# Keys in 8 MB loads: grouped query attention of one decoded token over a 32,768-row cache

## The chip, the cores and the metric

The kernel runs on one core of a Trainium2 chip. The metric is the device time of one execution in microseconds. A program takes it from three runs (median, lowest, highest); one more execution was recorded by the hardware profiler, and all rows of the profile are from that one.

## The reference

Two batch rows, one new token each. A layer norm of `x` feeds an attention block over a long key and value cache and a small dense block whose output gates it:

```python
xn = layernorm(x)                                  # (2, 1, 512)
q = (xn @ wq).reshape(2, 1, 32, 128)               # 32 query heads
# 8 key heads, each shared by 4 query heads; 32,768 cached rows of 128
scores = q . k_cache * 128 ** -0.5                 # k_cache (2, 8, 32768, 128) float32
o = softmax(scores) . v_cache                      # v_cache (2, 8, 32768, 128) float32
s = o.reshape(2, 1, 4096) @ wo                     # wo (4096, 512)
h = relu(xn @ w1 + b1) ** 2                        # w1 (512, 1792)
g = silu(h @ w2 + b2)                              # w2 (1792, 512)
out = x + s * g
```

All data are float32. The two caches are 268 MB each and make up nearly all of the 561 MB that are read.

## The kernel before

The work is cut into 16 *streams* `s`, one for each pair of key head and batch row, and each stream into 4 *chunks* of 8192 cache rows (4 MB). Chunk `n` is chunk `n % 4` of stream `n // 4`, for n from 0 to 63.

**Loads.** All bulk loads are issued by SP in one fixed order, the list `loads`, from a ring of four buffers of 32 KB for each of the 128 partitions (L56, tag "r"). A load goes out as soon as a buffer is free: `give()` frees one and calls `issue()`, which emits as many loads of the list as there is room for. The order is wq in two halves, then k0, k1, w1, k2, w2, k3, then keys and values in turn (k4, v0, k5, v1, ...), the last four value chunks, and wo in four parts, the last of which goes in four pieces (PIECES). A key load (`load_k`, L91) gives partition p 64 cache rows of 128 floats, one run of 32 KB in the cache; the partitions' runs start 128 KB apart, since all four chunks of a stream interleave by partition. A value load (`load_v`, L98) takes 4 MB in one piece, again with 32 KB for each partition.

**Scores** (`scores(n)`): DVE transposes the key chunk in 32x32 blocks into eight tiles `kt` (L246, eight instructions), PE multiplies them with the stream's queries `qz` (L251) into the PSUM tile `sc[t]`, and DVE takes the maximum (L255). The ring buffer of the keys is free after the eighth transpose. `set_q` (L232, POOL) lays out the queries of a stream.

**Softmax and probabilities.** `softmax(s)` runs after the stream's fourth chunk: the maximum over all (DVE, PE, DVE), then four exponentials on ACT (L272) into the tile `p`. `probs(s)` transposes `p` on PE (L286), copies it to `pT` (L287, ACT) and computes the reciprocals of the sums (L292 to L296). 

**Values** (`values(n)`): PE multiplies `pT` with a value chunk (L309) into `o_ps`. The value buffer is free after these matmuls. After the fourth chunk the stream's output is scaled and laid out (L316 to L329).

The main loop runs `n` from 0 to 67. In step n it emits `scores(n)`; the dense block's first layer in step 1 (`mlp_up`) and its second in step 2 (`mlp_down`); `probs` of the stream before in the first step of a stream; `softmax` of the stream in its fourth; and `values(n - 4)`. So values run four chunks behind scores. At the end PE multiplies with wo (L390), DVE applies the gate and adds x (L399, L400), and two small stores write the result. Each engine executes its instructions in the order in which they were emitted.

Of the kernel before, what the change touches and what calls it, by code (L numbers as in the profile page):

```python
# [9 lines left out]
F32 = mybir.dt.float32  # L10
# [4 lines left out]
P = 128  # L15
# [4 lines left out]

NG = 4
RUN = 64
CHUNK = P * RUN
NO = 16
BUFS = 4
NEG = -3.0e38
PIECES = ((0, 4), (4, 6), (6, 7), (7, 8))

# [2 lines left out]
def gqa_decode_kernel(ctx: ExitStack, tc: tile.TileContext, x, kc, vc, wq, wo, w1, b1, w2, b2, out):  # L33
    nc = tc.nc
    B, _, D = x.shape
# [4 lines left out]
    ND = D // P  # L40
# [11 lines left out]
    out2 = out.rearrange("b s d -> (b s) d")  # L52

    const = ctx.enter_context(tc.tile_pool(name="const", bufs=1))
    ring = ctx.enter_context(tc.tile_pool(name="ring", bufs=BUFS))
    ktpool = ctx.enter_context(tc.tile_pool(name="ktpool", bufs=8))  # L56
    work = ctx.enter_context(tc.tile_pool(name="work", bufs=2))
    pms = ctx.enter_context(tc.tile_pool(name="pms", bufs=2, space=bass.MemoryType.PSUM))
# [3 lines left out]
        return pms.tile([P, 512], F32, tag="ms", name=name)  # L62


    xt = const.tile([P, D], F32, name="xt")
    b1t = const.tile([NG, FG], F32, name="b1t")
    b2t = const.tile([1, D], F32, name="b2t")
    nc.vector.memset(xt, 0.0)
    nc.scalar.dma_start(xt[:B, :], x2)
    nc.scalar.dma_start(b1t, b1.rearrange("(g f) -> g f", g=NG))  # L70
# [8 lines left out]
    def rows(cache, s):  # L79
        hkv, b = divmod(s, B)  # L80
        return cache[b, hkv]

    def load_wq(i):
        t = ring.tile([P, 2, wq.shape[1]], F32, tag="r", name=f"wq{i}")
        nc.sync.dma_start(t, wq.rearrange("(p d) f -> p d f", p=P)[:, 2 * i:2 * i + 2, :])
        return t

    def load_k(m):
        s, u = divmod(m, NCH)
        t = ring.tile([P, RUN, DH], F32, tag="r", name=f"k{m}")  # L90
        nc.sync.dma_start(t, rows(kc, s).rearrange("(p t r) d -> p t r d", p=P, t=NCH)[:, u])  # L91
        return t

    def load_v(m):
        s, u = divmod(m, NCH)
        t = ring.tile([P, RUN, DH], F32, tag="r", name=f"v{m}")
        src = rows(vc, s)[u * CHUNK:(u + 1) * CHUNK].rearrange("(p r) d -> p r d", p=P)
        nc.sync.dma_start(t, src)  # L98
        return t

    def load_w1(_):
        t = ring.tile([P, ND, F], F32, tag="r", name="w1")
        nc.sync.dma_start(t, w1.rearrange("(p d) f -> p d f", p=P))
        return t

    def load_w2(_):
        t = ring.tile([P, FJ, D], F32, tag="r", name="w2")
        nc.sync.dma_start(t, w2.rearrange("(p j) e -> p j e", p=P))
        return t


    def load_wo(i):
        if i % 2 == 0:
            wide[i // 2] = ring.tile([P, 2, WG, D], F32, tag="r", name=f"wo{i // 2}")
        t = wide[i // 2][:, i % 2]
        src = wo[i * WG * P:(i + 1) * WG * P, :].rearrange("(p j) e -> p j e", p=P)
        if i < NWG - 1:
            nc.sync.dma_start(t, src)
        else:
            for j0, j1 in PIECES:  # L120
                nc.sync.dma_start(t[:, j0:j1, :], src[:, j0:j1, :])
        return t

    wide = {}
    NK = NS * NCH
    loads = [(1, load_wq, 0), (1, load_wq, 1)]
    for m in range(NK + NCH):
        if m < NK:
            loads.append((1, load_k, m))
        if m == 1:  # L130
            loads.append((1, load_w1, 0))
        if m == 2:
            loads.append((1, load_w2, 0))
        if m >= NCH:
            loads.append((1, load_v, m - NCH))
    loads += [(1 - i % 2, load_wo, i) for i in range(NWG)]
    free = [BUFS]
    done = [0]

    def issue():  # L140
        while done[0] < len(loads) and free[0] >= loads[done[0]][0]:
            bufs, f, a = loads[done[0]]
            free[0] -= bufs
            tiles[f, a] = f(a)
            done[0] += 1

    def take(f, a):
        return tiles.pop((f, a))

    def give():  # L150
        free[0] += 1
        issue()

    issue()
# [37 lines left out]
    nc.scalar.activation(st[:, 2:3], st[:, 1:2], AF.Sqrt)  # L192
    nc.vector.reciprocal(st[:, 3:4], st[:, 2:3])
    nc.vector.tensor_scalar(xn, xn, st[:, 3:4], None, op0=ALU.mult)  # L194
    xnT = const.tile([P, ND, P], F32, name="xnT")
    t_ps = misc("xnT_ps")
    for d in range(ND):
        nc.tensor.transpose(t_ps[:, d * P:(d + 1) * P], xn.rearrange("p (k d) -> p d k", d=ND)[:, d], ident)  # L198
    nc.vector.tensor_copy(xnT.rearrange("p a b -> p (a b)"), t_ps)  # L199


    for i in range(2):
        wqt = take(load_wq, i)
        for d2 in range(2):
            d = 2 * i + d2
            for f in range(2):
                for g in range(NG):
                    cc = f * NG + g
                    nc.tensor.matmul(sc[f][32 * g:32 * g + 32, :], xnT[:, d, 0:32],  # L209
                                     wqt[:, d2, cc * 512:(cc + 1) * 512], start=(d == 0), stop=(d == ND - 1))  # L210
        give()
    qT = const.tile([P, B, HKV, REP, 4], F32, name="qT")
    for f in range(2):
        for h in range(REP):
# [20 lines left out]
    rm, pr, pT, rs = {}, {}, {}, {}  # L235

    def scores(n):
        s, t = divmod(n, NCH)
        if t == 0:
            rm[s] = work.tile([P, NCH], F32, tag="rm4", name=f"rm4_{s}")  # L240
        kt = take(load_k, n)
        for e0 in range(0, 4, 2):
            kts = []
            for g in range(NG):
                r = ktpool.tile([P, 2, NO, 32], F32, tag="kt", name=f"kt{n}_{e0}_{g}")
                nc.vector.transpose(r.rearrange("p e o w -> p o e w"),  # L246
                                    kt[:, g * NO:(g + 1) * NO, e0 * 32:(e0 + 2) * 32].rearrange("p o (e w) -> p o e w", e=2))
                kts.append(r)
            for e in range(2):
                for g in range(NG):  # L250
                    nc.tensor.matmul(sc[t][32 * g:32 * g + 4 * REP, :], qz[s % 2][:, e0 + e, :],  # L251
                                     kts[g][:, e].rearrange("p o w -> p (o w)"),
                                     start=(e0 + e == 0), stop=(e0 + e == 3))
        give()
        nc.vector.tensor_reduce(rm[s][:, t:t + 1], sc[t], axis=AX.X, op=ALU.max)  # L255

    def softmax(s):
# [21 lines left out]

    def probs(s):  # L280
        p, lh = pr.pop(s)
        sb = work.tile([P, NG, 4, NO, REP], F32, tag="pT", name=f"pT{s}")
# [12 lines left out]
        r4 = work.tile([P, 4, REP], F32, tag="rs", name=f"rs{s}")  # L295
        nc.vector.tensor_mul(r4, selg[:, :4 * REP].rearrange("p (o h) -> p o h", h=REP),  # L296
                             r[:, None, :].to_broadcast([P, 4, REP]))
        rs[s] = r4
# [3 lines left out]
    def values(n):  # L302
# [3 lines left out]
        for i in range(NO // 4):  # L306
            for g in range(NG):
# [1 line left out]
                nc.tensor.matmul(o[32 * g:32 * g + 16, :], pT[s][:, g, a, 4 * i:4 * i + 4, :].rearrange("p o h -> p (o h)"),  # L309
                                 vt[:, lo:lo + 4, :].rearrange("p o d -> p (o d)"),  # L310
                                 start=(a == 0 and i == 0), stop=(a == NCH - 1 and i == NO // 4 - 1))
        give()
        if a == NCH - 1:
            hkv, b = divmod(s, B)
            o_sb = work.tile([P, 512], F32, tag="o_sb", bufs=1, name=f"o_sb{s}")
# [5 lines left out]
            nc.vector.tensor_copy(oT[:, hkv * REP:(hkv + 1) * REP, b], t_ps[:, :REP])  # L321
            if hkv % 2 == 1:
                i = hkv // 2
                m = work.tile([P, WG, P // WG], F32, tag="om", name=f"om{s}")
# [4 lines left out]
                nc.scalar.copy(oW[:, i, :, b], t_ps[:, :WG])  # L329


    hT, gate = const.tile([P, FJ, 32], F32, name="hT"), const.tile([P, DE], F32, name="gate")

    def mlp_up():
        wt = take(load_w1, 0)
# [6 lines left out]
        give()  # L342
# [7 lines left out]
    def mlp_down():  # L350
# [5 lines left out]
        for j in range(FJ):  # L356
            for g in range(NG):
                nc.tensor.matmul(y_ps[32 * g:32 * g + 32, :DE], hT[:, j, :], wt[:, j, g * DE:(g + 1) * DE],  # L358
                                 start=False, stop=(j == FJ - 1))
        give()  # L360
        e = work.tile([P, DE], F32, tag="e", name="e")
        nc.scalar.activation(e, y_ps[:, :DE], AF.Sigmoid)
        nc.vector.tensor_mul(gate, e, y_ps[:, :DE])


    for n in range(NK + NCH):
        s, t = divmod(n, NCH)
        if n < NK:
            if t == 0:
                set_q(s)  # L370
            scores(n)
        if n == 1:
            mlp_up()
        if n == 2:
            mlp_down()
        if s >= 1 and t == 0:
            probs(s - 1)
        if n < NK and t == NCH - 1:
            softmax(s)
        if n >= NCH:  # L380
            values(n - NCH)


    a_ps = sc[0]
# [9 lines left out]
        project(i, 0, WG)  # L394
    for j0, j1 in PIECES:
        project(NWG - 1, j0, j1)
    asb = work.tile([P, DE], F32, tag="e", name="a_sb")
    fin = const.tile([P, DE], F32, name="fin")
    nc.vector.tensor_mul(asb, gate, a_ps[:, :DE])  # L399
    nc.vector.tensor_add(fin, asb, xe)  # L400
# [25 lines left out]
```

## Time and profile before

| | |
|---|---|
| median of 3 runs | 1316.25 us (1316.2 to 1316.35) |
| the profiled execution | 1315.98 us |
| its span, first to last instruction | 1314.2 us |
| granted TensorE clock, mean | 0.861 of full |
| busy: PE, DVE, ACT | 946.4, 675.2, 107.5 us |
| read from HBM | 561.01 MB |

The page gives the span in 40 equal slices, a digit for each engine: its busy share in tenths. A row of instructions reads: line, engine, operation, tiles out<-in, sizes, count; in the timeline it is preceded by its start and its duration in us, and followed in brackets by the idle time ahead of it and what ended that. A name with q (SPq) is the engine's sequencer issuing a DMA. A DMA queue's row gives packets, MB, and the time of its packets as a share of 16 DMA engines. A row "DMA packets" counts all queues and says how many packets were small. The chain of waits goes back from the last instruction, at each step to what released it: its rows give start, duration and what.

### The profile page before, as it was taken

How to read it: one execution, taken by the hardware profiler on the slowest of the kernel's cores; microseconds unless marked ns; L12 is line 12 of the kernel's file. 1: busy time of each engine (PE TensorE's matmuls, PEld its weight loads, DVE VectorE, ACT ScalarE, POOL GpSimd, SP SyncE). 2: the span in 40 equal slices, each digit the busy share in tenths (PEclk: the TensorE clock that was granted, in tenths of full speed). 3: DMA queues.
4: the chain of work that ended last, by engine and by line, in shares of the span. 5: the costliest groups of instructions: out<-in, count | busy, mean ns of one | idle time of the engine just before them, and what ended most of it. 6: DMA issues, size and time to landing. Idle time of an engine off the chain costs nothing.

```text
span 1314.2 us, 11662 instructions
## 1 busy us (share of the span) xinstructions
PE 946.4 (72%) x5054; PEld 245.7 (19%) x5054; DVE 675.2 (51%) x778; ACT 107.5 (8%) x237; POOL 15.1 (1%) x76
## 2 busy tenths in 40 slices
PE   4777786876868677776776778586686767668666
PEld 1121121212112121111212112121211212112123
DVE  4765564553655465465454556355365546446510
ACT  0010000101001010100101001010100101010010
POOL 1000000000000000000000000000000000000000
PEclk9989888988888878887887988898887887888798
DMA  9999999999999999999999999999999999999997
GB/s 412 425 436 430 431 430 430 429 431 431 431 432 431 430 430 430 431 431 430 431 431 430 430 431 430 431 434 430 432 431 432 429 433 432 430 430 432 430 431 310
DMA packets 20113, 561.76 MB, mean 427 GB/s; under 512 B 2247, under 2 KB 2267, under 8 KB 2654
## 3 DMA queue, kind: packets, MB, share of 16 engines
q1 hardware_dynamic: 20024, 561.00, 99.3%
q8 instruction: 39, 0.64, 0.2%
q14 instruction: 12, 0.10, 0.0%
q10 hardware_dynamic: 38, 0.02, 0.0%
HBM read 561.01 MB, written 0.00 MB: 427 GB/s over the span
## 4 chain that ended last, share of the span: by engine, by line
DMA 76%; DVE 22%; PE 1%; issue 0%; ACTq 0%; DVEq 0%
DMA k<-in_A_k_cache 71%; DVE kt L246 22%; DMA v<-in_A_v_cache 2%; DMA wo<-in_A_wo 2%; PE sc L209 1%; DMA xt<-in_A_x 1%; PE y_ps L358 0%; PE sc L251 0%; PE xnT_ps L198 0%; DVE sq L189 0%; DVE xnT L199 0%; DVE st L190 0%; DVE st L186 0%; DVEq L246 0%; ACTq L70 0%
## 5 line engine op out<-in xcount | busy, mean ns | idle before, releaser
L251 PE MATMUL sc<-kt,qz 128*16 128x512 f32 x2048 | 605.6, 695 | 276.9 <-DVE kt L246 256.2
L246 DVE STREAM_TRANSPOSE kt<-k 128x1024 f32<-128x1024 f32 x512 | 584.3, 1207 | 288.3 <-DMA k<-in_A_k_cache 288.3
L309 PE MATMUL o_ps<-v,pT 128*16 128x512 f32 x2048 | 272.9, 604 | 11.5 <-DMA v<-in_A_v_cache 11.5
L251 PEld LDWEIGHTS sc<-kt,qz 128*16 128x16 f32 x2048 | 94.1, 100 | 768.9 <-DVE kt L246 652.0
L272 ACT ACTIVATE p<-sc,nm 128x512 f32<-128x512 f32 x64 | 68.8, 1198 | 1025.4 <-DVE nm L268 1025.4
L255 DVE TENSOR_REDUCE rm<-sc 128x1 f32<-128x512 f32 x64 | 44.3, 692 | 126.3 <-PE sc L251 126.3
L309 PEld LDWEIGHTS o_ps<-v,pT 128*16 128x16 f32 x2048 | 66.1, 98 | 169.9 <-issue 152.0
L286 PE MATMUL pT_ps<-ident,p 128*128 128x128 f32 x256 | 52.1, 381 | 0.1
L286 PEld LDWEIGHTS pT_ps<-ident,p 128*128 128x128 f32 x256 | 46.3, 205 | 5.6 <-issue 2.6
L320 PE MATMUL oT_ps<-rs,o_sb 128*128 128x4 f32 x128 | 19.2, 273 | 34.3 <-ACT o_sb L316 34.3
L275 DVE TENSOR_REDUCE l<-l 128x1 f32<-128x4 f32 x16 | 2.5, 154 | 66.9 <-ACT p L272 66.9
L294 DVE RECIPROCAL r<-l_ps 128x4 f32<-128x4 f32 x16 | 2.9, 183 | 56.5 <-PE l_ps L292 56.5
L321 DVE COPY oT<-oT_ps 128x4 f32<-128x4 f32 x16 | 2.6, 163 | 51.7 <-PE oT_ps L320 51.7
L287 ACT COPY pT<-pT_ps 128x256 f32<-128x256 f32 x64 | 23.9, 373 | 45.7 <-PE pT_ps L286 45.1
L320 PEld LDWEIGHTS oT_ps<-rs,o_sb 128*128 128x128 f32 x128 | 17.8, 215 | 48.3 <-ACT o_sb L316 48.3
L232 POOL COPY qz<-qT 32x16 f32<-32x16 f32 x64 | 12.8, 200 | 1081.4 <-PE sc L251 1051.2
L261 PE MATMUL mx_ps<-ident,rm 128*128 128x128 f32 x16 | 5.1, 319 | 15.8 <-DVE rm L259 15.8
L272 ACT ACTIVATION_READ_ACCUMULATOR p<-sc,nm 128x1 f32 x64 | 14.6, 228 | 0.0
L316 ACT COPY o_sb<-o_ps 128x512 f32<-128x512 f32 x16 | 9.7, 604 | 31.0 <-PE o_ps L309 31.0
L198 PE MATMUL xnT_ps<-ident,xn 128*128 128x128 f32 x4 | 1.1, 428 | 15.2 <-DVE xn L194 15.2
L390 PE MATMUL sc<-wo,oW 128*32 128x128 f32 x256 | 8.8, 275 | 3.4 <-DMA wo<-in_A_wo 3.3
L209 PE MATMUL sc<-wq,xnT 128*32 128x512 f32 x64 | 10.0, 792 | 0.8 <-DVE xnT L199 0.8
(67 smaller groups left out, 107.5 us busy)
## 6 DMA issues: line engine op xcount, KB each, us to landing
k<-in_A_k_cache SPq DMA_DIRECT2D x64, 4096.0 KB, 29.6
v<-in_A_v_cache SPq DMA_DIRECT2D x64, 4096.0 KB, 29.6
wq<-in_A_wq SPq DMA_DIRECT2D x2, 4096.0 KB, 12.2
w<-in_B_w SPq DMA_DIRECT2D x2, 3584.0 KB
wo<-in_A_wo SPq DMA_DIRECT2D x3, 2048.0 KB
wo<-in_A_wo SPq DMA_DIRECT2D x1, 1024.0 KB
wo<-in_A_wo SPq DMA_DIRECT2D x1, 512.0 KB
wo<-in_A_wo SPq DMA_DIRECT2D x2, 256.0 KB, 29.4
```

The costliest lines, as they stand in the source:

```text
L209: nc.tensor.matmul(sc[f][32 * g:32 * g + 32, :], xnT[:, d, 0:32], wqt[:, d2, cc * 512:(cc + 1) * 512], start=(d == 0), stop=(d == ND - 1))
L232: nc.gpsimd.tensor_copy(qz[s % 2][32 * a:32 * a + 32, :, a * REP:(a + 1) * REP], qT[32 * a:32 * a + 32, b, hkv].rearrange("p h e -> p e h"))
L246: nc.vector.transpose(r.rearrange("p e o w -> p o e w"), kt[:, g * NO:(g + 1) * NO, e0 * 32:(e0 + 2) * 32].rearrange("p o (e w) -> p o e w ...
L251: nc.tensor.matmul(sc[t][32 * g:32 * g + 4 * REP, :], qz[s % 2][:, e0 + e, :], kts[g][:, e].rearrange("p o w -> p (o w)"), start=(e0 + e = ...
L255: nc.vector.tensor_reduce(rm[s][:, t:t + 1], sc[t], axis=AX.X, op=ALU.max)
L272: nc.scalar.activation(p[:, :, :, t], sc[t].rearrange("p (o w) -> p o w", w=32), AF.Exp, bias=nm, scale=SCALE, accum_out=l4[:, t:t + 1])
L286: nc.tensor.transpose(t_ps[:, j * P:(j + 1) * P], p[:, 4 * i + j].rearrange("p w t -> p (w t)"), ident)
L287: nc.scalar.copy(sb[:, :, :, 4 * i:4 * i + 4, :].rearrange("p g a o h -> p o g a h"), t_ps.rearrange("p (o g y) -> p o g y", o=4, g=NG)[:, ...
L309: nc.tensor.matmul(o[32 * g:32 * g + 16, :], pT[s][:, g, a, 4 * i:4 * i + 4, :].rearrange("p o h -> p (o h)"), vt[:, lo:lo + 4, :].rearran ...
L316: nc.scalar.copy(o_sb, o)
L320: nc.tensor.matmul(t_ps[:, :REP], o_sb[:, i * DH:(i + 1) * DH], r4[:, i, :], start=(i == 0), stop=(i == 3))
L390: nc.tensor.matmul(a_ps[32 * g:32 * g + 32, :DE], oW[:, i, j, :], wot[i][:, j, g * DE:(g + 1) * DE], start=(i == 0 and j == 0), stop=(i == ...
```

## The change

- The ring goes. Keys get one tile of three slots of 32 KB (`kslots`), values, wq, w1 and w2 a pool of two buffers of 32 KB (`vpool`).
- From the second stream on, keys are loaded two chunks at a time: 8 MB, with one run of 64 KB for each partition. Load m (chunks 2m and 2m + 1) fills slots 0 and 1 when m is even, 1 and 2 when it is odd. The chunk in slot 1, which the next load needs first, is processed first; `TS` says which quarter of a stream's rows a chunk is.
- The first stream's keys are loaded in four halves of such a load (`load_half`, 4 MB, 32 KB runs), with w1 after the second and w2 after the fourth.
- After each 8 MB key load from the third on come two value loads. At the end v60 and v61 go into key slots 0 and 1, and wo into slots 2 and 0.
- A load waits for a named event instead of a count of free buffers: key load m for `("s", 2m - 2)`, the transposes of the first chunk of the load before; value load j for `("v", j - 2)`; the list is still in one order on SP.
- `mlp_down` moves from step 2 to step 3, `probs(s)` from the first step of the next stream to the end of the stream's own fourth step, behind `softmax(s)` and `values(n - 4)`.
- To make room, x, b2, xnT and hT share the memory of the tile `p`, and `pT`, `om` and `e` have one buffer instead of two.

```diff
+TS = (1, 0, 2, 3)
...
-    ring = ctx.enter_context(tc.tile_pool(name="ring", bufs=BUFS))
+    vpool = ctx.enter_context(tc.tile_pool(name="vpool", bufs=2))
...
+    first = work.tile([P, 4, D], F32, tag="p", bufs=1, name="first")
+    xt, b2t = first[:, 0], first[0:1, 1]
...
+    def key_slot(n):
+        return n // 2 % 2 + TS[n % NCH] % 2
+
+    def load_half(n):
+        t = TS[n]
+        nc.sync.dma_start(kslots[:, key_slot(n)], rows(kc, 0).rearrange("(p t r) d -> p t (r d)", p=P, t=NCH)[:, t])
+
     def load_k(m):
-        s, u = divmod(m, NCH)
-        t = ring.tile([P, RUN, DH], F32, tag="r", name=f"k{m}")
-        nc.sync.dma_start(t, rows(kc, s).rearrange("(p t r) d -> p t r d", p=P, t=NCH)[:, u])
-        return t
+        s, u = divmod(m, 2)
+        nc.sync.dma_start(kslots[:, u:u + 2, :].rearrange("p i f -> p (i f)"),
+                          rows(kc, s).rearrange("(p u r) d -> p u (r d)", p=P, u=2)[:, u])
 
     def load_v(m):
         s, u = divmod(m, NCH)
-        t = ring.tile([P, RUN, DH], F32, tag="r", name=f"v{m}")
-        src = rows(vc, s)[u * CHUNK:(u + 1) * CHUNK].rearrange("(p r) d -> p r d", p=P)
-        nc.sync.dma_start(t, src)
+        if m - NK + NCH in (0, 1):
+            t = kslots[:, m - NK + NCH].rearrange("p (r d) -> p r d", d=DH)
+        else:
+            t = vpool.tile([P, RUN, DH], F32, tag="v", name=f"v{m}")
+        nc.sync.dma_start(t, rows(vc, s)[u * CHUNK:(u + 1) * CHUNK].rearrange("(p r) d -> p r d", p=P))
         return t
...
-    loads = [(1, load_wq, 0), (1, load_wq, 1)]
-    for m in range(NK + NCH):
-        if m < NK:
-            loads.append((1, load_k, m))
-        if m == 1:
-            loads.append((1, load_w1, 0))
-        if m == 2:
-            loads.append((1, load_w2, 0))
-        if m >= NCH:
-            loads.append((1, load_v, m - NCH))
-    loads += [(1 - i % 2, load_wo, i) for i in range(NWG)]
+    kslots = const.tile([P, 3, RUN * DH], F32, name="kslots")
+    loads = [(None, load_wq, 0), (None, load_wq, 1), (None, load_half, 0), (None, load_half, 1), (("q", 0), load_w1, 0),
+             (("s", 0), load_half, 2), (None, load_half, 3), (("q", 1), load_w2, 0)]
+    for m in range(2, NK // 2):
+        loads.append((("s", 2 * m - 2), load_k, m))
+        for j in (2 * m - 4, 2 * m - 3):
+            loads.append((("w", j) if j < 2 else ("v", j - 2), load_v, j))
+    loads += [(("s", NK - 3), load_v, NK - 4), (("s", NK - 2), load_v, NK - 3),
+              (("v", NK - 6), load_v, NK - 2), (("v", NK - 5), load_v, NK - 1)]
+    loads += [(("s", NK - 1), load_wo, 0), (("s", NK - 1), load_wo, 1), (("v", NK - 4), load_wo, 2), (("v", NK - 4), load_wo, 3)]
...
-        s, t = divmod(n, NCH)
-        if t == 0:
+        s, t = n // NCH, TS[n % NCH]
+        if n % NCH == 0:
...
-        kt = take(load_k, n)
+        kt = kslots[:, key_slot(n)].rearrange("p (r d) -> p r d", d=DH)
...
-        give()
+        give("s", n)
...
-        if n == 2:
+        if n == NCH - 1:
             mlp_down()
-        if s >= 1 and t == 0:
-            probs(s - 1)
-        if n < NK and t == NCH - 1:
+        if n < NK and i == NCH - 1:
             softmax(s)
         if n >= NCH:
             values(n - NCH)
+        if n < NK and i == NCH - 1:
+            probs(s)
```

More of the change, by code (lines that the diff above doesn't have):

```diff
@@ L26 @@
 NO = 16
-BUFS = 4
+TS = (1, 0, 2, 3)
 NEG = -3.0e38
@@ L62, in misc @@
         return pms.tile([P, 512], F32, tag="ms", name=name)
-    xt = const.tile([P, D], F32, name="xt")
+    first = work.tile([P, 4, D], F32, tag="p", bufs=1, name="first")
+    xt, b2t = first[:, 0], first[0:1, 1]
     b1t = const.tile([NG, FG], F32, name="b1t")
-    b2t = const.tile([1, D], F32, name="b2t")
     nc.vector.memset(xt, 0.0)
@@ L83, in load_wq @@
     def load_wq(i):
-        t = ring.tile([P, 2, wq.shape[1]], F32, tag="r", name=f"wq{i}")
+        t = vpool.tile([P, 2, wq.shape[1]], F32, tag="v", name=f"wq{i}")
         nc.sync.dma_start(t, wq.rearrange("(p d) f -> p d f", p=P)[:, 2 * i:2 * i + 2, :])
         return t
+    def key_slot(n):
[3 more added lines that the diff above has]
+        nc.sync.dma_start(kslots[:, key_slot(n)], rows(kc, 0).rearrange("(p t r) d -> p t (r d)", p=P, t=NCH)[:, t])
     def load_k(m):
-        s, u = divmod(m, NCH)
-        t = ring.tile([P, RUN, DH], F32, tag="r", name=f"k{m}")
-        nc.sync.dma_start(t, rows(kc, s).rearrange("(p t r) d -> p t r d", p=P, t=NCH)[:, u])
-        return t
+        s, u = divmod(m, 2)
+        nc.sync.dma_start(kslots[:, u:u + 2, :].rearrange("p i f -> p (i f)"),
+                          rows(kc, s).rearrange("(p u r) d -> p u (r d)", p=P, u=2)[:, u])
     def load_v(m):
         s, u = divmod(m, NCH)
-        t = ring.tile([P, RUN, DH], F32, tag="r", name=f"v{m}")
-        src = rows(vc, s)[u * CHUNK:(u + 1) * CHUNK].rearrange("(p r) d -> p r d", p=P)
-        nc.sync.dma_start(t, src)
+        if m - NK + NCH in (0, 1):
[3 more added lines that the diff above has]
+        nc.sync.dma_start(t, rows(vc, s)[u * CHUNK:(u + 1) * CHUNK].rearrange("(p r) d -> p r d", p=P))
         return t
     def load_w1(_):
-        t = ring.tile([P, ND, F], F32, tag="r", name="w1")
+        t = vpool.tile([P, ND, F], F32, tag="v", name="w1")
         nc.sync.dma_start(t, w1.rearrange("(p d) f -> p d f", p=P))
@@ L106, in load_w2 @@
     def load_w2(_):
-        t = ring.tile([P, FJ, D], F32, tag="r", name="w2")
+        t = vpool.tile([P, FJ, D], F32, tag="v", name="w2")
         nc.sync.dma_start(t, w2.rearrange("(p j) e -> p j e", p=P))
@@ L113, in load_wo @@
         if i % 2 == 0:
-            wide[i // 2] = ring.tile([P, 2, WG, D], F32, tag="r", name=f"wo{i // 2}")
+            wide[i // 2] = kslots[:, 2 - i].rearrange("p (i j e) -> p i j e", i=2, j=WG)
         t = wide[i // 2][:, i % 2]
@@ L125, in gqa_decode_kernel @@
     NK = NS * NCH
-    loads = [(1, load_wq, 0), (1, load_wq, 1)]
-    for m in range(NK + NCH):
-        if m < NK:
-            loads.append((1, load_k, m))
-        if m == 1:
-            loads.append((1, load_w1, 0))
-        if m == 2:
-            loads.append((1, load_w2, 0))
-        if m >= NCH:
-            loads.append((1, load_v, m - NCH))
-    loads += [(1 - i % 2, load_wo, i) for i in range(NWG)]
-    free = [BUFS]
+    kslots = const.tile([P, 3, RUN * DH], F32, name="kslots")
[8 more added lines that the diff above has]
+    loads += [(("s", NK - 1), load_wo, 0), (("s", NK - 1), load_wo, 1), (("v", NK - 4), load_wo, 2), (("v", NK - 4), load_wo, 3)]
+    past = {None}
     done = [0]
     def issue():
-        while done[0] < len(loads) and free[0] >= loads[done[0]][0]:
-            bufs, f, a = loads[done[0]]
-            free[0] -= bufs
+        while done[0] < len(loads) and loads[done[0]][0] in past:
+            _, f, a = loads[done[0]]
             tiles[f, a] = f(a)
@@ L148, in take, with give @@
         return tiles.pop((f, a))
-    def give():
-        free[0] += 1
+    def give(*event):
+        past.add(event)
         issue()
@@ L194, in gqa_decode_kernel @@
     nc.vector.tensor_scalar(xn, xn, st[:, 3:4], None, op0=ALU.mult)
-    xnT = const.tile([P, ND, P], F32, name="xnT")
+    xnT = first[:, 2].rearrange("p (d b) -> p d b", d=ND)
     t_ps = misc("xnT_ps")
@@ L198, in gqa_decode_kernel @@
         nc.tensor.transpose(t_ps[:, d * P:(d + 1) * P], xn.rearrange("p (k d) -> p d k", d=ND)[:, d], ident)
-    nc.vector.tensor_copy(xnT.rearrange("p a b -> p (a b)"), t_ps)
+    nc.vector.tensor_copy(first[:, 2], t_ps)
     for i in range(2):
@@ L210, in gqa_decode_kernel @@
                                      wqt[:, d2, cc * 512:(cc + 1) * 512], start=(d == 0), stop=(d == ND - 1))
-        give()
+        give("q", i)
     qT = const.tile([P, B, HKV, REP, 4], F32, name="qT")
@@ L253, in scores @@
                                      start=(e0 + e == 0), stop=(e0 + e == 3))
-        give()
+        give("s", n)
         nc.vector.tensor_reduce(rm[s][:, t:t + 1], sc[t], axis=AX.X, op=ALU.max)
@@ L281, in probs @@
         p, lh = pr.pop(s)
-        sb = work.tile([P, NG, 4, NO, REP], F32, tag="pT", name=f"pT{s}")
+        sb = work.tile([P, NG, 4, NO, REP], F32, tag="pT", bufs=1, name=f"pT{s}")
         for i in range(NO // 4):
@@ L311, in values @@
                                  start=(a == 0 and i == 0), stop=(a == NCH - 1 and i == NO // 4 - 1))
-        give()
+        give("v", n)
         if a == NCH - 1:
@@ L323, in values @@
                 i = hkv // 2
-                m = work.tile([P, WG, P // WG], F32, tag="om", name=f"om{s}")
+                m = work.tile([P, WG, P // WG], F32, tag="om", bufs=1, name=f"om{s}")
                 nc.vector.tensor_mul(m, oT[:, i * WG:(i + 1) * WG, b:b + 1].to_broadcast([P, WG, P // WG]),
@@ L329, in values @@
                 nc.scalar.copy(oW[:, i, :, b], t_ps[:, :WG])
-    hT, gate = const.tile([P, FJ, 32], F32, name="hT"), const.tile([P, DE], F32, name="gate")
+    hT, gate = first[:, 3, :FJ * 32].rearrange("p (j b) -> p j b", j=FJ), const.tile([P, DE], F32, name="gate")
     def mlp_up():
@@ L341, in mlp_up @@
                                  start=False, stop=(d == ND - 1))
-        give()
+        give("w", 0)
         hr = work.tile([P, FG], F32, tag="tmp", name="hr")
@@ L359, in mlp_down @@
                                  start=False, stop=(j == FJ - 1))
-        give()
-        e = work.tile([P, DE], F32, tag="e", name="e")
+        give("w", 1)
+        e = work.tile([P, DE], F32, tag="e", bufs=1, name="e")
         nc.scalar.activation(e, y_ps[:, :DE], AF.Sigmoid)
@@ L366, in gqa_decode_kernel @@
     for n in range(NK + NCH):
-        s, t = divmod(n, NCH)
+        s, i = divmod(n, NCH)
         if n < NK:
-            if t == 0:
+            if i == 0:
                 set_q(s)
@@ L396, in gqa_decode_kernel @@
         project(NWG - 1, j0, j1)
-    asb = work.tile([P, DE], F32, tag="e", name="a_sb")
+    asb = work.tile([P, DE], F32, tag="e", bufs=1, name="a_sb")
     fin = const.tile([P, DE], F32, name="fin")
@@ L412 @@
     from concourse.bass_utils import run_bass_kernel_spmd
-    nc = bacc.Bacc("TRN2", target_bir_lowering=False, num_devices=1)
+    nc = bacc.Bacc("TRN2", target_bir_lowering=False, num_devices=1, dynamic_dma_scratch_size=1024)
     arrays, args = {}, {}
```

## The prediction

> **What bounds the kernel now.** I read the page first: the slices, the queues and the chain of waits.
>
> ```profile
> span 1314.2 us, 11662 instructions
> PE   4777786876868677776776778586686767668666
> DVE  4765564553655465465454556355365546446510
> DMA  9999999999999999999999999999999999999997
> q1 hardware_dynamic: 20024, 561.00, 99.3%
> HBM read 561.01 MB, written 0.00 MB: 427 GB/s over the span
> DMA 76%; DVE 22%; PE 1%; issue 0%; ACTq 0%; DVEq 0%
> k<-in_A_k_cache SPq DMA_DIRECT2D x64, 4096.0 KB, 29.6
> ```
>
> No engine fills its row, while the DMA row is full in every slice but the last: q1, the queue of SP's loads, takes 99.3% of the 16 DMA engines' span. The chain's 22% for DVE is misleading. It follows the release of one buffer to the load that refills it, and that load then stands 29.6 us between issue and landing although it moves only 4 MB. The chain in order of time and the transfers of the steady part show why:
>
> ```profile
> 382.42 9.14 DVE kt L246 x8
> 391.57 29.60 DMA k<-in_A_k_cache
> ...
> 1055.15 29.61 DMA k<-in_A_k_cache
> DMA packets 17328, 504.20 MB, mean 431 GB/s; under 512 B 1916, under 2 KB 1916, under 8 KB 1916
> q1 hardware_dynamic: 17283, 503.55, 100.1%
> q8 instruction: 34, 0.56, 0.2%
> ```
>
> The chain steps from one key load to the next but one. Between the two rows shown are 17 such steps, (1055.15 - 391.57)/17 = 39.03 us each; four loads (two of keys, two of values) go in that time, so a load takes 9.76 us. Of the 29.6 us from issue to landing, some 20 are thus spent behind two other loads. The last three rows are the window from 100 to 1270 us: the engines are 100% busy there, and 1916 tiny packets (some 16 for each load) are the only ones under 8 KB. The time is therefore bytes plus whatever each packet costs beside its bytes. The bytes do not change. I need the cost of a packet.
>
> **Price of a packet.** Two windows at the end hold smaller packets (wo in 16, 8, 4 and 2 KB runs):
>
> ```profile
> DMA packets 460, 6.29 MB, mean 419 GB/s; under 512 B 54, under 2 KB 54, under 8 KB 80
> q1 hardware_dynamic: 460, 6.29, 98.6%
> DMA packets 551, 2.39 MB, mean 239 GB/s; under 512 B 67, under 2 KB 67, under 8 KB 425
> q1 hardware_dynamic: 549, 2.36, 58.0%
> q1 hardware_dynamic: 291, 1.05, 51.8%
> DMA  7997967879278165444656536645565744343100
> ```
>
> The first pair is 1285 to 1300 us, the second 1300 to 1310, the single row 1304 to 1309; the last row shows 1300 to 1310 in 40 slices of 0.25 us. Let each data packet cost a, its share of the tiny packets included, and each MB b. Steady window: 100.1% of 16 x 1170 us is 18,739 us for 17283 - 1916 = 15,367 data packets and 503.55 MB. Window 1300 to 1310: 58.0% of 160 us is 92.8 us for 549 - 67 = 482 packets and 2.36 MB. Taken together, b = 37.21 - 30.52a (us per MB), and 482a + 2.36b = 92.8 gives a = 0.0121 us. The window 1285 to 1300 (98.6% of 240 us, 406 packets, 6.29 MB) gives 0.0120. So a data packet costs 12 ns beyond its bytes on the mean engine, within about 1 ns for the rounding of the rows.
>
> The end is not set by the mean engine. From 1304 to 1309 us only 51.8% of the engines' time is used: about half of them have finished the last load and the others have not. The share missing is 1.4% of 15 us in the first window, 0.2 us, and 42% less 1.4 points for an instruction fetch over 10 us, 4.1 us, of which 0.5 lies after the last packet (two empty slices). The last engines end about 3.8 us after the mean. Each engine moves the same bytes in (20024 - 2247)/16 = 1111 data packets (the page has 2247 under 512 B), so if the lag is a packet's cost, it is 3.4 ns each, and the last engines pay 15.4 ns. Against that, records that overlap (100.1% and 0.2%) could make 12 ns too much by 0.3% of the 1219 ns of one packet, 3.7 ns. I take 13.5 ns, between the mean and the last engines, since the last set the end; the bounds are 8.4 and 15.4.
>
> **What the change takes away.** The first stream's four key chunks keep 32 KB runs; the other 60 chunks go in 30 loads of 128 packets of 64 KB instead of 60 loads of 128 packets of 32 KB. That is 30 x 128 = 3840 packets fewer, 240 for each engine: 240 x 13.5 ns = 3.24 us (2.0 to 3.7). There are 30 x 16 tiny packets fewer, 30 for each engine. No view prices them alone; they lie between 0 and a data packet's 12 ns, so 0 to 0.36 us, and I take 0.2. A steady window has no packet over 32 KB. One of 64 KB could cost what two do (gain 0 beside the tiny ones) or one; the three sizes above lie on one line, so I take one. Sum: 3.4 us.
>
> The Trainium skill, "DMA: Bandwidth & Descriptors", section "Why small descriptors are slow (HBM only)", names a fixed overhead of about 3 cycles per packet; at the 850 MHz of its section "Where 436 GB/s comes from" that is an estimate of 3.5 ns, and the sum would be 0.8 us, lost in the noise. The 12 ns of the windows speak against it.
>
> **What it moves: the refill of the keys.** Today any buffer released lets the next 4 MB go. Afterwards an 8 MB key load waits for one thing: the DVE transposes of the first half of the key load before it, which free the middle slot. SP is in order, so both value loads behind it wait as well. Cover is what is queued at that time: the pair of values.
>
> ```profile
> 617.10 9.13 DVE L246 STREAM_TRANSPOSE kt<-k 128x1024 f32<-128x1024 f32 x8 [7.62 <-DMA k<-in_A_k_cache]
> 618.40 9.78 PE L251 MATMUL sc<-kt,qz 128*16 128x512 f32 x32 [6.22 <-DVE kt L246]
> 626.25 0.33 SPq L91 DMA_DIRECT2D k<-in_A_k_cache  x1
> 629.40 3.63 PE L309 MATMUL o_ps<-v,pT 128*16 128x512 f32 x32
> 641.21 0.17 DVE L296 TENSOR_TENSOR rs<-selg,r 128x16 f32<-128x16 f32 x1
> 641.30 9.12 DVE L246 STREAM_TRANSPOSE kt<-k 128x1024 f32<-128x1024 f32 x8
> ```
>
> DVE starts on keys as they land, takes 9.13 us, and SP issues at 626.25, 0.02 us after it. The values cover 2 x 9.76 = 19.5 us, so the new load is in the queue 10.4 us before the DMA engines would run dry. The worst place is the stream's last step, where softmax and now probs stand on DVE ahead of the next transposes. Counted from the landing of that stream's last 8 MB: PE does scores, values and scores, about 1.3 + 9.8 + 3.6 + 9.8 = 24.5 us. From the end of scores (628.18) to the next stream's transposes (641.30) is 13.1 us in the trace, with softmax, values and probs in it as after the change. Sum 37.6 us; the next keys land 39.0 us after the last. DVE is ready just in time, and the 10.4 us are still behind that. The value loads wait for values two loads back, done a whole pair earlier. I cost the refill at nothing; without the cover each us would be paid at up to 15 stream heads.
>
> **Start and end.** The first five loads keep their order, so the third key chunk lands as before:
>
> ```profile
> 0.74 1.98 SPq L85 DMA_DIRECT2D wq<-in_A_wq  x2
> 33.13 9.09 DVE L246 STREAM_TRANSPOSE kt<-k 128x1024 f32<-128x1024 f32 x8
> 42.25 0.33 SPq L108 DMA_DIRECT2D w<-in_B_w  x1
> 61.49 9.13 DVE L246 STREAM_TRANSPOSE kt<-k 128x1024 f32<-128x1024 f32 x8 [0.32 <-DMA k<-in_A_k_cache]
> 72.40 3.22 PE L358 MATMUL y_ps<-w,hT 128*32 128x128 f32 x100
> ```
>
> That chunk waits for the first chunk's transposes (42.2 us) and is wanted at about 61.5 - 9.8 = 51.7: margin 9.5 us. The first 8 MB load waits for the third chunk's transposes, 70.6 us, with the fourth chunk and w2 still to run until 61.5 + 9.8 + 8.5 = 79.8: margin 9.2 us. mlp_down one chunk later frees a value slot needed at 79.8 + 19.5 + 9.8 = 109 us, and ends at about 61.5 + 9.8 + 9.1 + 2 + 4 = 86; the first softmax, whose probabilities now lie where mlp_down reads, is put off by those 4 us, under the 10.4 of cover. At the end the order v, v, v, v, wo stays; v60 and v61 take key slots long free, and the last steps are the same:
>
> ```profile
> 1309.99 0.43 PE L390 MATMUL sc<-wo,oW 128*32 128x128 f32 x8 [0.21 <-DMA wo<-in_A_wo]
> 1310.80 0.29 DVE L400 TENSOR_TENSOR fin<-a_sb,xe 128x128 f32<-128x128 f32 x1
> ```
>
> Both cost nothing. The other edits (the tiles that share space, fewer spare buffers) touch nothing that waits: pT with one buffer is written by probs only after the values that read it, which stand before it in every step; om and e are written 8 and 2 times in all.
>
> The profiled execution took 1315.98 us (span 1314.2 and 1.8 around it), the median is 1316.25. 1315.98 - 3.4 = 1312.6 profiled, and with the 0.27 us between them 1312.8 as the time.
>
> **Rivals.**
> 1. *No packet is saved, or it costs next to nothing.* A 64 KB run goes as two packets, or costs as two. For it: nothing over 32 KB is in the trace. Against it: a packet's cost comes out the same from windows of 16 KB and of mostly 2 to 4 KB. Only the tiny packets go: 1316.25 - 0.2 = 1316.0. By the three cycles of the Trainium skill quoted above the time would be 1315.3; a fifth of this rival's chance is for that.
> 2. *The refill runs dry (slower).* Its place is SP's wait for the middle slot, and it decides when the transposes end over 19.5 us after the landing, 9.1 in the trace: a delay of 10.4 us. Were DVE held for 12 us at each of 15 stream heads, the DMA engines would stand for 15 x 1.6 = 24 us: 1312.8 + 24 = 1337. For it: softmax, values and probs now stand in one piece before a stream's first transposes. Against it: the sum of 37.6 us, and the 7.62 us of idle DVE ahead of its set today.
> 3. *Long runs move slower.* At 1% more for each byte of the 60 chunks, 60 x 9.76 x 1% = 5.9 us are lost and 3.4 won: 1318.7. It decides at 0.6%. For it: each engine then stays in one place of the cache twice as long, which no row here prices. Against it: b is the same in windows of short and of long runs.
> 4. *A load has a cost of its own.* 4.19 MB at b/16 = 2.30 us per MB are 9.66 us, which leaves 0.10 of the 9.76; 8 packets of 12 ns make the same 0.10. What the rounding and the late engines leave is 8 x 4.4 ns = 0.035 us; 30 loads fewer would bring 1.1 us more: 1311.7, and 1311.1 with the upper prices of the packets (3.7 + 0.36 + 1.1 = 5.2). The Trainium skill, same page, section "Anatomy of one DMA — SWDGE (gpsimd) path", gives each DMA a fixed part of about 2.0 us; if that lay on the path, 30 loads would be an estimated 60 us and the time 1256. By that rule loads could not follow each other at 9.76 us, so the trace disagrees for loads that stand queued; it has 0.01 of this rival's chance.
>
> **Chances.** The forecast, one fixed cost per packet, 0.64: its own range is 1312.2 (3.7 + 0.36 saved) to 1314.2 (2.0 saved). Rival 1: 0.19. Rival 2: 0.05. Rival 3: 0.08. Rival 4: 0.04. A change of under 0.2% (2.6 us) can hardly be told from none here, so 1313.6 is the line. Faster by more: the forecast but for 0.06 at its edge, and rival 4: 0.62. Within: rival 1, that edge, and a rival 3 of under 1%, 0.01: 0.26. Slower: 0.12. The range goes from rival 4's end, 1311.1, over the forecast to rival 1 with its rounding, 1316.2, and leaves out rivals 2 and 3.
>
> **What would show it.** Right: q1's packets fall from 20,024 to about 20,024 - 3840 - 480 = 15,704 with 561.00 MB unchanged; the steady windows stay at 100% and rise from 431 to about 432 GB/s; key loads still land far later after issue than an 8 MB transfer takes (over 28 us against 19.5). Wrong: 20,000 packets (rival 1); a 9 in the DMA row that turns 8 or less, or a wait of DVE's transposes for keys with a steady window below 99% (rival 2); a lower rate at 100% busy (slower packets).

## The result and the profile after

The changed kernel takes 1313.82 us (median of 20 runs, 1313.67 to 1315.02) against 1316.22 (20 runs, 1316.0 to 1316.55) before: ratio 0.9982, 95% interval 0.9975 to 0.9989. That is 2.4 us or 0.18% less, where 3.4 us were forecast. All but one of the 20 times lie below all 20 of before by over 1.9 us.

The page of the changed kernel, with the rows that answer to those shown of before:

```profile
span 1312.1 us, 11652 instructions
DMA  9999999999999999999999999999999999999997
q1 hardware_dynamic: 15704, 561.00, 99.3%
kslots<-in_A_k_cache SPq DMA_DIRECT2D x30, 29.8
```

The queue moves the same 561.00 MB in 15,704 packets, the number forecast, and is as full as before. The 30 key loads of 8 MB land 29.8 us after their issue (median), though 8 MB take 19.5: they still stand queued behind other loads.

The transfers of the window from 100 to 1270 us, and the two windows at the end (1285 to 1300 and 1300 to 1310 us):

```profile
DMA packets 13183, 505.12 MB, mean 432 GB/s; under 512 B 1456, under 2 KB 1456, under 8 KB 1456
q1 hardware_dynamic: 13140, 504.50, 100.0%
...
q1 hardware_dynamic: 575, 6.25, 98.7%
...
DMA  8856637533656555464557444443310000000000
q1 hardware_dynamic: 399, 1.63, 39.7%
```

In the steady window the engines are busy throughout, and the rate is 432 GB/s instead of 431. The last packet ends at 1307.5 us (ten empty slices of 0.25 us), 2 us earlier than before. With 0.4% and 0.6% for q8 (instruction fetches) in these two windows, the share missing is 0.9% of 15 us and 59.7% of 10 us less the 2.5 us that are empty, 0.1 + 3.5 = 3.6 us: the last engines lag behind the mean as they did before (3.8).

The timeline at a stream's end, DVE and SP alone:

```profile
606.32 11.38 DVE L254 STREAM_TRANSPOSE kt<-kslots 128x1024 f32<-128x1024 f32 x10 [18.70 <-DMA kslots<-in_A_k_cache]
615.48 0.33 SPq L99 DMA_DIRECT2D kslots<-in_A_k_cache  x1
641.21 0.17 DVE L304 TENSOR_TENSOR rs<-selg,r 128x16 f32<-128x16 f32 x1
645.31 11.38 DVE L254 STREAM_TRANSPOSE kt<-kslots 128x1024 f32<-128x1024 f32 x10 [3.93 <-DMA kslots<-in_A_k_cache]
```

SP issues the next key load 615.48 - 606.32 = 9.2 us after the last one landed, and the new keys are there 39 us after it, as the two values in between and the load itself take. At the stream's end DVE has finished probs at 641.4, 35 us after the landing, and then idles 3.93 us until the keys land.

### The profile page after: what moved, and what is told of

Its sections match the earlier page's. It is cut to its first block, busy times and chain, and to the rows that moved or that the text cites. A ratio compares the mean times of both kernels' runs of the same rounds, so it can differ in the third digit from the quotient of the medians.

```text
span 1312.1 us, 11652 instructions
## 1 busy us (share of the span) xinstructions
PE 845.6 (64%) x5054; PEld 244.8 (19%) x5054; DVE 670.2 (51%) x778; ACT 107.4 (8%) x237; POOL 15.1 (1%) x76
## 3 DMA queue, kind: packets, MB, share of 16 engines
q1 hardware_dynamic: 15704, 561.00, 99.3%
## 4 chain that ended last, share of the span: by engine, by line
DMA 73%; DVE 20%; issue 4%; PE 2%; ACT 0%; ACTq 0%; DVEq 0%
DMA kslots<-in_A_k_cache 69%; DVE kt L254 19%; DMA kslots<-in_A_wo 3%; PE sc L217 1%; DMA first<-in_A_x 1%; PE sc L398 0%; PE o_ps L317 0%; ACT p L280 0%; PE pT_ps L294 0%; DVE qr L224 0%; PE qT_ps L228 0%; PE sc L259 0%; DVE rm L263 0%; PE oT_ps L328 0%; PE xnT_ps L206 0%
## 5 line engine op out<-in xcount | busy, mean ns | idle before, releaser
L259 PE MATMUL sc<-kt,qz 128*16 128x512 f32 x2048 | 531.1, 663 | 371.5 <-DVE kt L254 356.1
L254 DVE STREAM_TRANSPOSE kt<-kslots 128x1024 f32<-128x1024 f32 x512 | 583.6, 1207 | 342.9 <-DMA kslots<-in_A_k_cache 342.9
L317 PE MATMUL o_ps<-v,pT 128*16 128x512 f32 x1984 | 264.0, 601 | 10.4 <-DMA v<-in_A_v_cache 10.3
L317 PEld LDWEIGHTS o_ps<-v,pT 128*16 128x16 f32 x1984 | 61.9, 97 | 162.6 <-issue 145.3
L398 PE MATMUL sc<-kslots,oW 128*32 128x128 f32 x256 | 9.9, 310 | 3.4 <-DMA kslots<-in_A_wo 3.4
L217 PE MATMUL sc<-wq,first 128*32 128x512 f32 x64 | 9.9, 789 | 0.8 <-DVE first L207 0.8
```

The costliest lines, as they stand in the source:

```text
L254: nc.vector.transpose(r.rearrange("p e o w -> p o e w"), kt[:, g * NO:(g + 1) * NO, e0 * 32:(e0 + 2) * 32].rearrange("p o (e w) -> p o e w ...
L398: nc.tensor.matmul(a_ps[32 * g:32 * g + 32, :DE], oW[:, i, j, :], wot[i][:, j, g * DE:(g + 1) * DE], start=(i == 0 and j == 0), stop=(i == ...
```

## The experiments

All are edits of the changed kernel. The first four were compared with the same runs of before (1316.12 us).

**Two loads instead of one** (e1). Only the load itself is split:

```diff
-        nc.sync.dma_start(kslots[:, u:u + 2, :].rearrange("p i f -> p (i f)"),
-                          rows(kc, s).rearrange("(p u r) d -> p u (r d)", p=P, u=2)[:, u])
+        for i in range(2):
+            nc.sync.dma_start(kslots[:, u + i, :],
+                              rows(kc, s).rearrange("(p t r) d -> p t (r d)", p=P, t=NCH)[:, 2 * u + i])
```

> The changed kernel, but each 8 MB key load is issued as two 4 MB loads of 32 KB runs at the same place in the order and behind the same wait: 3840 data packets and 480 tiny packets come back (q1 20,024), all else stays. Theory 1 (a fixed cost per packet): 240 x 10 to 12 ns for each engine come back, about 1316.2 us. Rival (the new order, slots and waits brought the gain): 1313.8 us as the changed kernel.

Measured: 1316.23 us, ratio to before 1.0 (0.9991 to 1.0009). The whole gain is gone, with the slots, the order, the waits, probs and mlp_down all left as changed. They cost and bring nothing together; the gain is in the packets or in the number of loads.

**One load, short runs** (e2). It tells these two apart:

```diff
-TS = (1, 0, 2, 3)
+TS = (2, 0, 1, 3)
...
+        return (1, 0, 1, 2)[n % NCH]
...
+        nc.sync.dma_start(kslots[:, u:u + 2, :],
+                          rows(kc, s).rearrange("(p i u r) d -> p u i (r d)", p=P, i=2, u=2)[:, u])
```

> The changed kernel, still one 8 MB load for two key chunks, but the two chunks of a load are now quarters 0 and 2 or 1 and 3 of the stream's rows, so that each partition gets two runs of 32 KB instead of one of 64 KB: q1 19,544 packets, the same 111 instructions on SP. Theory 1 (packets): 1316.0 us, 2.2 to 2.9 above the changed kernel. Rival A (fewer loads, each with a cost of its own): 1313.8 us. Rival B (order and waits): 1313.8 us.

Measured: 1315.99 us, ratio to before 0.9999 (0.999 to 1.0008). With 8 MB in each load but 32 KB in each packet, 2.17 us of the gain are lost: 240 packets for each engine at 9.0 ns. (The 95% intervals of the changed kernel, up to 0.9989, and of this one, from 0.999, do not overlap.) What 30 loads more cost is the difference to e1, 0.24 us, 8 ns for each of the 30 tiny packets of an engine. That difference is near the spread of the runs.

**Keys in 8 KB runs** (e3), so that the price can be read from a larger lever:

```diff
+PAD = 8
...
-    kslots = const.tile([P, 3, RUN * DH], F32, name="kslots")
+    kslots = const.tile([P, 12, NO * DH + PAD], F32, name="kslots")
...
+        nc.sync.dma_start(kslots[:, 4 * u:4 * u + 8, :NO * DH],
+                          rows(kc, s).rearrange("(p u g o) d -> p u g (o d)", p=P, u=2, o=NO)[:, u])
...
```

> The changed kernel with all keys in runs of 8 KB: the key slots have a gap of 32 bytes after every 8 KB in each partition, the loads and waits stay. 64 x 512 packets for keys instead of 4352, 28,416 more, 1776 for each engine. Theory 1 with 12 ns for each: 21 us more, 1335 us; with the 10 ns that the result suggests 1331.6. If the late engines pay 15.4 ns as the prediction had it: 1341. A cost that does not go with packets: 1313.8.

Measured: 1328.56 us, ratio to before 1.0094 (1.0081 to 1.0108). 14.74 us for 1776 packets of each engine are 8.3 ns each, and against e2 12.57 us for 1536 are 8.2. The gaps are in the key slots alone, and a partition's rows in the cache are still one piece of 64 KB: the cost goes with the number of packets, not with the length of a run in the cache. The price is nearly the same from 64 KB down to 8 KB, but lower than I had expected. The rows of this run say why, and what the late engines have to do with it. The first is the window from 100 to 1270 us, then come 1300 to 1310 and 1310 to 1325:

```profile
q1 hardware_dynamic: 38921, 498.67, 100.5%
...
q1 hardware_dynamic: 286, 4.18, 98.1%
...
DMA  8989989899997673835546554555644100000000
q1 hardware_dynamic: 677, 3.49, 56.3%
```

The share is 100.5%, against 100.0% of the changed kernel. 16 engines can't be busier than 100%, so the records of packets overlap, and the more packets, the more: 0.5% of 1170 us is 5.9 us for (38,921 - 1431)/16 - (13,140 - 1456)/16 = 1613 packets more for each engine (1431 tiny ones by that window's answer), 3.6 ns each. A price from busy time is too high by that. And the lag at the end is 1.9% of 10 us and, with 0.9% for q8, 42.8% of 15 us less eight empty slices of 0.375, 0.2 + 3.4 = 3.6 us. With 2.8 times as many packets (44,120 in the page's q1 row, against 15,704) it has not grown, so it is no price of packets.

**The middle slot last** (e4). The chunk in the shared slot is processed second, so the next key load waits for both chunks:

```diff
-TS = (1, 0, 2, 3)
+TS = (0, 1, 3, 2)
...
-             (("s", 0), load_half, 2), (None, load_half, 3), (("q", 1), load_w2, 0)]
+             (None, load_half, 2), (("s", 1), load_half, 3), (("q", 1), load_w2, 0)]
...
-        loads.append((("s", 2 * m - 2), load_k, m))
+        loads.append((("s", 2 * m - 1), load_k, m))
...
-    loads += [(("s", NK - 3), load_v, NK - 4), (("s", NK - 2), load_v, NK - 3),
+    loads += [(("s", NK - 3), load_v, NK - 4), (("s", NK - 1), load_v, NK - 3),
```

> The changed kernel, but the chunk in the middle slot is processed second, so that the next key load waits for the transposes of both chunks. Theory (10.4 us of queued values cover the wait): the second eight transposes take 9.1 us or a little more, the cover shrinks to about 1 us less SP's issue and start of some 1.5 us, so 0 to 1 us are lost at each of 30 loads, more at stream heads: 1314 to 1345 us, with gaps in the DMA row. Rival (the queue is deep in any case): 1313.8 us.

Measured: 1383.9 us, ratio to before 1.0516 (1.0502 to 1.053), 70 us above the changed kernel and beyond the range that I had given. The page's q1 row, the chain in order of time, the timeline, and the DMA row of 612 to 622 us in slices of 0.25:

```profile
q1 hardware_dynamic: 15704, 561.00, 95.5%
...
599.69 0.02 issue
...
618.48 21.82 DMA kslots<-in_A_k_cache
640.30 0.03 issue
...
618.48 0.33 SPq L99 DMA_DIRECT2D kslots<-in_A_k_cache  x1
...
DMA  2993409930699306993003300000099070000000
```

The load is issued 18.8 us after the landing of the one before. Two values take 19.5 us, so counted from that landing 0.7 us of work should have been left. The DMA row, which counts a packet in the slice in which it starts, shows that most engines had none. A value packet takes 1.22 us (9.76 / 8); after 616.75 only two of them start, after 617.75 none, and the first packets of the new load start after 619.25 (in the window from 618.48 to 620.48 the first 19 slices of 0.05 us are empty, so 0.95 us after the issue). A load lands when the last of the 16 engines has finished it; the others are by then ahead and run out earlier than the count says. The landing comes 21.82 us after the issue, though 8 MB take 19.5: 0.95 us of the 2.3 between them lie ahead of the first packet, the rest in engines that do not finish together and in the landing itself. The two loads' landings are 640.30 - 599.69 = 40.6 us apart instead of 39.0, and 40.6 to 42 at others: about 2.3 us at each of 30 loads, 70 us. The 1.5 us that I had put for issue and start were enough; what I had wrong was to count the 16 engines as one, all at work until the cover ends and all done 19.5 us after a load starts.

The Trainium skill, "DMA: Bandwidth & Descriptors", section "Anatomy of one DMA — SWDGE (gpsimd) path", gives a DMA issued by GpSimd a fixed part of about 2.0 us. These loads are issued by SP; of a fixed part the trace shows the 0.95 us ahead of the first packet and no other share by itself. In e1, where 30 loads more stand queued, they cost 0.24 us in all.

**More loads for the values** (e5), 64 partitions in each:

```diff
-        nc.sync.dma_start(t, rows(vc, s)[u * CHUNK:(u + 1) * CHUNK].rearrange("(p r) d -> p r d", p=P))
+        src = rows(vc, s)[u * CHUNK:(u + 1) * CHUNK].rearrange("(p r) d -> p r d", p=P)
+        for p0 in (0, 64):
+            nc.sync.dma_start(t[p0:p0 + 64], src[p0:p0 + 64])
```

> The changed kernel, but each of the 64 value loads is issued as two loads of 64 partitions (2 MB each): the same data packets of 32 and 64 KB, 64 loads more, so 64 x 16 tiny packets more, 64 for each engine (q1 16,728). Theory (a queued load costs only its tiny packets; the two kernels with and without the 30 extra loads differed by 0.24 us, 8 ns each): 64 x 8 ns = 0.5 us, 1314.3 us. Rival (a load has a fixed part on the path): by the Trainium skill's 2 us for each DMA 128 us more; anything above 1316 speaks for it.

Measured: 2346.5 us (median of 6 runs, 2248 to 2395), far beyond both. As a test of the number of loads it failed, since the way that the loads were cut changed something else. The window from 150 to 250 us:

```profile
GB/s 419 419 419 275 170 210 197 197 210 210 210 210 210 210 210 210 210 203 210 328 131 341 419 419 419 419 419 419 288 170 197 197 210 223 210 184 236 210 210 203
q1 hardware_dynamic: 744, 26.12, 100.0%
```

The engines are 100% busy, yet the rate falls from 419 to some 210 GB/s and back. The page of this kernel has 87.5% for q1 over its span, so gaps came on top. Why is open here; whether it was the number of loads or their 64 partitions was the next question.

**Value loads cut the other way** (e8): two loads over all partitions, 16 KB runs.

```diff
...
+        for r0 in (0, RUN // 2):
+            nc.sync.dma_start(t[:, r0:r0 + RUN // 2], src[:, r0:r0 + RUN // 2])
```

> The changed kernel, but each of the 64 value loads is issued as two loads over all 128 partitions with 16 KB runs (2 MB each): 64 loads more, as in the kernel with 64 partitions for each load, and 8192 data packets and 1024 tiny ones more (512 and 64 for each engine; q1 24,920). Theory (9 ns for a data packet, 8 ns for a tiny one, nothing else for a queued load): 4.6 + 0.5 = 5.1 us more, 1318.9 us. Rival (64 loads more have a price of their own, which made the other kernel slow): far above, by 2 us for each 1442. If 1318.9, it was the 64 partitions of a load that made the other kernel slow, not the number of its loads.

Measured: 1318.75 us, ratio to its runs of before (1316.2) 1.0019 (1.001 to 1.0028), 4.93 us above the changed kernel where 5.1 were expected. 64 loads more cost their packets and nothing that can be seen beside; e5's loss belongs to loads of 64 partitions.

**Long runs for the values** (e7). Two value slots side by side, one load of 8 MB for two chunks, and in every second step the values of both:

```diff
+        t = (kslots if m == NK - NCH else vslots)[:, 0:2]
+        nc.sync.dma_start(t.rearrange("p i f -> p (i f)"),
+                          rows(vc, s)[u * CHUNK:(u + 2) * CHUNK].rearrange("(p r) d -> p (r d)", p=P))
...
-        for j in (2 * m - 4, 2 * m - 3):
-            loads.append((("w", j) if j < 2 else ("v", j - 2), load_v, j))
+        loads.append((("w", 1) if m == 2 else ("v", 2 * m - 5), load_v, 2 * m - 4))
...
+        if n >= NCH and i % 2:
+            values(n - NCH - 1)
             values(n - NCH)
...
```

> The changed kernel with the value chunks, too, in 8 MB loads of 64 KB runs; the values of two chunks are multiplied one after the other in every second step. In this layout of the cache the rows of a 64 KB value run do not belong to the key rows that the probabilities were made from, so this kernel pairs wrong rows, and its time alone counts. 32 x 128 = 4096 data packets fewer (256 for each engine) and 32 x 16 tiny ones. Theory (9 ns for each packet that goes, 8 ns for each tiny one): 2.3 + 0.3 = 2.6 us less, 1311.2 us. Rival (the gain belongs to the keys, whose 32 KB runs lay 128 KB apart): 1313.8 us. If the refill of the values has no cover left: over 1316.

Measured: 1311.36 us, ratio to before (1316.14) 0.9962 (0.995 to 0.9975), 2.46 us below the changed kernel where 2.6 were expected. Page and steady window:

```profile
q1 hardware_dynamic: 11096, 561.00, 99.2%
...
q1 hardware_dynamic: 8667, 505.09, 99.9%
```

4608 packets fewer once more, and the same gain again. It does not belong to the keys or to the place of their runs in the cache. A version that can be used was not found: the row after a 32 KB run can be the next one either for the key load's partition or for the value load's, not for both, in the way that scores are turned into probabilities here. This was reasoned, not tried. Long runs for the first stream and wq would save 24 packets for each engine, about 0.2 us by the same price, and were not tried either.

The prices side by side, against the changed kernel (data and tiny packets for each engine):

| kernel | more data packets | more tiny ones | time, us | difference |
|---|---|---|---|---|
| long values | -256 | -32 | 1311.36 | -2.46 |
| changed | 0 | 0 | 1313.82 | |
| short runs | 240 | 0 | 1315.99 | 2.17 |
| two loads | 240 | 30 | 1316.23 | 2.41 |
| before | 240 | 30 | 1316.22 | 2.40 |
| value halves | 512 | 64 | 1318.75 | 4.93 |
| 8 KB runs | 1776 | 0 | 1328.56 | 14.74 |

8.3 ns for a data packet and 8 for a tiny one give every row within 0.2 us, on keys and on values. The medians of before that belong to these runs are 1316.22, 1316.12, 1316.14 and 1316.20 us, so a difference between two sets of runs is good to about 0.1 us. The granted TensorE clock does not go with the times: in the profiled executions it is 0.87 in two loads and 0.86 in long values, 0.81 in the changed kernel and 0.82 in short runs, so either clock has a slower and a faster kernel.

## Why the prediction was right, and where its size was off

- *What bounds the kernel*: right. The DMA engines set the time, the bytes stay, and only a packet's fixed cost could go. Two loads in the place of one bring 1316.23 back with everything else changed.
- *The price of a packet*: the term that was mis-sized. I took 13.5 ns, from 12 on the mean engine and 3.4 for the last engines. The first was too high because the records overlap; I had named that as the lower bound, 8.4 ns, and not used it, and 8.3 to 9.0 is what the runs show. The second was wrong: the lag of the last engines stays at 3.6 us with 2.8 times as many packets. With the smaller price the change came out at 1313.82, on the other side of the 1313.6 that the prediction had drawn as its line: 0.62 stood on a faster time and 0.26 on one such as this. What makes some engines late remains open; no view here tells the 16 engines apart. One candidate is in the traces: each of the kernels in the table has 39 instruction fetches of 16 KB (q8), some 41.5 us of engine time in all, and their durations repeat from eighth to eighth, as if they went round eight engines. That would put these eight 2.6 us behind the mean, an estimate (41.5 / 16). No run tests it.
- *The packets saved*: right, 3840 data and 480 tiny ones; one 64 KB run is one packet, and rival 1 falls. 240 x 9.0 ns and 30 x 8 ns are 2.2 + 0.24 = 2.4 us, and with the 8.3 ns of the 8 KB runs 2.2. The 3.5 ns estimated from the three cycles of the Trainium skill, "DMA: Bandwidth & Descriptors", section "Why small descriptors are slow (HBM only)", would have been 0.8 us: the measurement is about 2.5 times that price.
- *The tiny packets*: 0.2 us taken, 0.24 measured.
- *The refill*: right that it costs nothing, and the rows of the sum came out nearly as worked out: issue 9.2 us after the landing, DVE free 35 us after it where I had 37.6. But the 10.4 us of cover were counted from a landing, which is the end of the last engine, down to an empty queue, without the start of a load. The leading engines had less: in the packet records of the changed kernel the first engine turns to a new key load 7.7 us after its issue in the early loads and only 1.6 us after it at the last one, and 0.95 us of that is the start. What it would cost if the leading engines alone ran dry was not tested. The middle slot last, issued 9.6 us later after a landing, shows where rival 2 decides: with 0.7 us left by the count, some 2.3 us are lost at each load.
- *Long runs move slower* (rival 3): falls. The keys and the values both gain by the price of the packets, at 100% busy.
- *A load's own cost* (rival 4): none that can be seen while it is queued (30 loads 0.24 us, 64 loads inside a sum that is met within 0.2 us); where it is not queued, its start of 0.95 us shows.
- *Start and end*: nothing, as said; e1 with the changed start and end is at 1316.23.

## What to carry to other kernels

Where the DMA engines are full, the time is bytes plus packets: count the packets that a change removes for each engine and multiply by a price taken from a run with many more of them, not from busy shares, which count the overlap of packet records twice. A larger load is worth its longer runs, not its smaller number of issues, as long as a load always stands queued; free its slot early enough. The start took 0.95 us here, and with the middle slot last most engines were out of work over 1 us before a count from landings said so. What to process first is then part of the memory plan: the chunk whose slot the next load needs.

## What the runs showed of the hardware that was not expected

Loads of 64 partitions move at half the rate: some 210 GB/s with all 16 engines busy all the time, against 419 for the 8 MB key loads of 128 partitions beside them. Their packets have 32 KB, as those of the changed kernel's value loads have. The kernel with such value loads took 2346 us. The same number of loads over all partitions took 1318.75. What the engines share when half of the partitions are written was not tested.
